# LayerScale with a residual on one Trainium2 core: head blocks of 4 or of 6 rows

## The chip, the cores and the metric

The kernel runs on one core of one Trainium2 chip. Its time is the device time of one execution in microseconds, and the time quoted is the median over several executions. The engines that matter here are the vector engine (DVE), which does the arithmetic, the two engines that issue transfers (SP, the sync engine, and ACT, the scalar engine), and the core's 16 DMA engines, which move the data between the chip's memory (DRAM) and the core's on-chip memory (128 partitions). SP's transfers appear in the profile as queue q1, ACT's as queue q10.

## The reference

```python
B, S, D = 1024, 16, 512
# x and y: [B, S, D] bfloat16; gamma: [D] bfloat16
def reference(x, y, gamma):
    return x + gamma * y
```

Flattened, x and y are 16384 rows of 512 values, 16.78 MB each, and the output has the same size. So 33.56 MB are read and 16.78 MB written, and for each element there is one multiplication and one addition.

## The kernel before

**Tiling.** The 16384 rows are dealt to the 128 partitions, 128 rows to each. In what follows a "row" is a row of one partition: 512 bf16 values, 1 KB. `BLOCKS` (line 7) cuts these 128 rows into three blocks. Within a block, `rows_of` (line 65) gives each partition one stretch of DRAM that has no gaps, as long as the block has rows: partition p of a 64-row block reads 64 KB, and partition p+1 reads the 64 KB after it. The whole of y stays in `y_sb` (128 rows per partition), is multiplied and added to in place, and is stored from there. x passes through the smaller `x_sb`; the last number of an x entry is the row of `x_sb` at which it is put, and an x load that overwrites rows of an earlier one waits until the additions that read those have been done (`frees`, line 102).

**Queues.** The order of the transfers is written out by hand. `SP` (line 12) and `ACT` (line 20) list them as (kind, first row, row behind the last), where kind is y, x, g (gamma) or s (a store). SP issues y rows 0 to 4, y 4 to 68, x 4 to 68, y 68 to 128, x 68 to 120, x 120 to 128. ACT issues x rows 0 to 4, gamma, and then the stores of rows 4 to 68, 0 to 4 and 68 to 128. The first two of SP and the first of ACT (`EARLY`, line 22) are put at the start of the program. What follows them on each engine waits for `HOLD`, the landing of y's head (line 24): the tensor engine waits for it (line 147) and releases SP, ACT and DVE by one semaphore each (line 149). The stores wait for `RELEASE`, the landing of x rows 68 to 120 (line 26), and each for the additions of its rows.

**Arithmetic.** `PIECES` (line 9) cuts the 128 rows into pieces of 8, 16, 44, 52 and 8 rows, one DVE instruction each for the multiplication (line 180) and for the addition (line 189). Piece 0 is rows 0 to 8 and so takes in the head and the beginning of the second block. Before that, gamma's row is spread over the partitions by one matmul with a row of ones (line 152) and copied to `gamma_sb` (line 154). The order of DVE's work is

```python
DVE = [('m', 0), ('m', 1), ('m', 2), ('a', 2), ('a', 0), ('a', 1), ('m', 3), ('m', 4), ('a', 3), ('a', 4)]
```

The addition of piece 2 (rows 24 to 68) comes first of the additions because x rows 68 to 120 are put over the places of x rows 24 to 68 in `x_sb`.

Of the kernel before, what the change touches and what calls it, by code (L numbers as in the profile page):

```python
# [3 lines left out]

BLOCKS = [4, 64, 60]

PIECES = [8, 16, 44, 52, 8]


SP = [
    ('y', 0, 4),
    ('y', 4, 68),
    ('x', 4, 68, 4),
    ('y', 68, 128),
    ('x', 68, 120, 24),
    ('x', 120, 128, 0),
]
ACT = [('x', 0, 4, 0), ('g',), ('s', 4, 68), ('s', 0, 4), ('s', 68, 128)]  # L20

EARLY = (2, 1)

HOLD, AHEAD = ('y', 0, 4), (2, 1)

RELEASE = ('x', 68, 120, 24)

# [10 lines left out]
def kernel(  # L38
# [22 lines left out]
    dt = xf.dtype  # L61
    edges = [sum(BLOCKS[:c]) for c in range(len(BLOCKS) + 1)]
    assert edges[-1] == rows

    def rows_of(t, a, b):

        c = max(c for c in range(len(BLOCKS)) if edges[c] <= a)
        assert b <= edges[c + 1]
# [6 lines left out]
    y_sb = nc.alloc_sbuf_tensor("y_sb", [P, rows, D], dt).ap()  # L75
    x_loads = [w for w in ACT + SP if w[0] == "x"]
    y_loads = [w for w in SP + ACT if w[0] == "y"]
    stores = [w for w in SP + ACT if w[0] == "s"]
    for loads in (x_loads, y_loads, stores):
# [33 lines left out]
    def ring(eng, what, n_early, n_ahead):  # L113

        known, went = 0, False
        for k, w in enumerate(what):
            kind = w[0]
            if k == n_ahead:
                _take(s_held[eng], 1, eng)
            need = frees(w) if kind == "x" else pieces_of(w[1], w[2]) + list(w[3:]) if kind == "s" else []  # L120
            need = max((order[c] + 1 for c in need), default=0)
            if kind == "s" and not went:
                _take(s_go, 1, eng)
                went = True
            if need > known:
                eng.wait_ge(s_add, need)
                known = need
            if kind == "g":
                i = eng.dma_start(out=gamma_row, in_=gamma.unsqueeze(0)).then_inc(s_gamma, 16)
            elif kind == "x":  # L130
                to = x_sb[:, w[3] : w[3] + w[2] - w[1], :]
                i = eng.dma_start(out=to, in_=rows_of(xf, w[1], w[2])).then_inc(s_load[w], 16)
            elif kind == "y":
                r = slice(w[1], w[2])
                i = eng.dma_start(out=y_sb[:, r, :], in_=rows_of(yf, w[1], w[2])).then_inc(s_load[w], 16)
            else:
                r = slice(w[1], w[2])
                i = eng.dma_start(out=rows_of(of, w[1], w[2]), in_=y_sb[:, r, :]).then_inc(s_out, 16)
            if k < n_early:
                early.append(i.ins)  # L140

    ring(nc.sync, SP, EARLY[0], AHEAD[0])
    ring(nc.scalar, ACT, EARLY[1], AHEAD[1])

# [89 lines left out]
```

## Time and profile before

| | |
|---|---|
| median of 3 runs | 119.76 us (119.75 to 119.79) |
| span of the profiled execution | 118.2 us (118.227 in the trace) |
| what lies around the span, if the median is taken for it | 1.53 us |
| DVE busy | 70.1 us |
| bytes moved | 50.33 MB, mean 426 GB/s over the span |

The profile gives for each DMA engine's unit of work (a "packet", here one partition's stretch) its start, its length and its size. Collected by transfer, in the order in which they run, in us from the start of the span:

| transfer | rows | bytes of one packet | packets per DMA engine | first packet starts | last engine done | median packet, ns |
|---|---|---|---|---|---|---|
| load y | 0 to 4 | 4096 | 8 | 1.38 | 3.43 | 159 |
| load x | 0 to 4 | 4096 | 8 | 2.59 | 4.37 | 159 |
| load y | 4 to 68 | 65536 | 8 | 4.03 | 23.89 | 2422 |
| load x | 4 to 68 | 65536 | 8 | 23.41 | 43.23 | 2420 |
| load y | 68 to 128 | 61440 | 8 | 42.75 | 61.38 | 2269 |
| load x | 68 to 120 | 53248 | 8 | 60.90 | 77.09 | 1966 |
| load x | 120 to 128 | 8192 | 8 | 76.65 | 79.55 | 309 |
| store | 4 to 68 | 65536 | 8 | 79.11 | 98.87 | 2418 |
| store | 0 to 4 | 4096 | 8 | 98.43 | 100.11 | 159 |
| store | 68 to 128 | 61440 | 8 | 99.67 | 118.23 | 2267 |

Besides, each transfer ends on each engine with a 4-byte packet of 9 ns, its semaphore. Gamma is a packet of 1024 bytes of 46 ns on one engine, at 9.00, and its semaphore comes at 11.50. Packets that follow each other on an engine overlap by 3 ns in these records where nothing holds them up. "Last engine done" is the end of the slowest engine; the fastest is some 0.33 to 0.47 us earlier throughout, so the next transfer starts on the fast engines before the last one is done on the slow ones.

### The profile page before, as it was taken

The numbers are of one execution on the slowest core, as the hardware profiler recorded it, in microseconds if no ns is written. First come the engines' busy times: TensorE is split into PE (matmuls) and PEld (weight loads), VectorE is DVE, ScalarE is ACT, GpSimd is POOL, SyncE is SP. The second block draws the span as 40 slices with busy tenths as digits, with TensorE's granted clock in tenths as the row PEclk, the third lists the DMA queues.
The fourth block names the chain that finished last, engine by engine and source line by source line (L and its number), as shares of the span: only waits on it lengthen the run. The fifth ranks groups of instructions, "written<-read, shape, count | busy, mean of one in ns | idle before, by whom it ended". The sixth has DMA issues, their size and how long they took to land. (4 is left out here: it accounts for less than half of the span.)

```text
span 118.2 us, 91 instructions
## 1 busy us (share of the span) xinstructions
PE 0.6 (0%) x1; PEld 0.1 (0%) x1; DVE 70.1 (59%) x12; POOL 0.2 (0%) x4
## 2 busy tenths in 40 slices
PE   0000100000000000000000000000000000000000
PEld 0000000000000000000000000000000000000000
DVE  0000200089999969999999999999999900000000
POOL 0000000000000000000000000000000000000000
DMA  6999889988899879879969696898899889799793
GB/s 248 461 666 399 355 355 399 665 355 355 355 599 466 355 333 624 374 333 499 499 288 576 288 576 288 360 637 355 355 576 488 355 355 510 333 582 416 333 499 166
DMA packets 1442, 50.33 MB, mean 426 GB/s; under 512 B 161, under 2 KB 162, under 8 KB 546
## 3 DMA queue, kind: packets, MB, share of 16 engines
q1 hardware_dynamic: 864, 33.03, 64.8%
q10 hardware_dynamic: 578, 17.30, 33.9%
HBM read 33.56 MB, written 16.78 MB: 426 GB/s over the span
## 5 line engine op out<-in xcount | busy, mean ns | idle before, releaser
L180 DVE TENSOR_TENSOR y_sb<-y_sb,gamma_sb 128x4096 bf16<-128x4096 bf16 (+3 forms) x5 | 34.7, 6981 | 10.9 <-DVEq L35 10.9
L189 DVE TENSOR_TENSOR y_sb<-x_sb,y_sb 128x4096 bf16<-128x4096 bf16 (+3 forms) x5 | 34.7, 6981 | 1.2 <-DVEq L35 1.1
L154 DVE CAST gamma_sb<-gamma_ps 128x512 bf16<-128x512 f32 x1 | 0.7, 692 | 10.2 <-DVEq L35 10.2
L146 DVE MEMSET ones_row<- 1x128 bf16 x1 | 0.2, 165 | 2.0 <-PEq L51 2.0
L152 PE MATMUL gamma_ps<-gamma_row,ones_row 1*128 1x512 bf16 x1 | 0.6, 581 | 11.6 <-PEq L35 11.6
L152 PEld LDWEIGHTS gamma_ps<-gamma_row,ones_row 1*128 1x128 bf16 x1 | 0.1, 101 | 11.6 <-issue 11.6
L218 POOL MEMSET const-bfloat16-1.0<- 128x1 bf16 x1 | 0.1, 101 | 0.0
L218 POOL MEMSET const-uint8-127<- 128x1 uint8 x1 | 0.1, 101 | 0.0
L218 POOL MEMSET const-float32-0.0<- 128x1 f32 x1 | 0.1, 98 | 0.2 <-issue 0.2
L218 POOL MEMSET const-float32-1.0<- 128x1 f32 x1 | 0.1, 98 | 0.0
## 6 DMA issues: line engine op xcount, KB each, us to landing
y_sb<-in_y_dram SPq DMA_DIRECT2D x1, 7680.0 KB, 57.3
out_dram<-y_sb ACTq DMA_DIRECT2D x1, 7680.0 KB, 23.8
x_sb<-in_x_dram SPq DMA_DIRECT2D x1, 6656.0 KB, 21.7
x_sb<-in_x_dram SPq DMA_DIRECT2D x1, 1024.0 KB, 22.0
y_sb<-in_y_dram SPq DMA_DIRECT2D x1, 512.0 KB, 3.4
x_sb<-in_x_dram ACTq DMA_DIRECT2D x1, 512.0 KB, 4.2
out_dram<-y_sb ACTq DMA_DIRECT2D x1, 512.0 KB, 22.3
y_sb<-in_y_dram SPq DMA_DIRECT2D x1, 23.4
```

Of the source, the lines that this page charges most:

```text
L146: nc.vector.memset(ones_row, 1.0).then_inc(s_ones, 1)
L152: nc.tensor.matmul(gamma_ps, ones_row, gamma_row, start=True, stop=True).then_inc(s_ps, 1)
L154: nc.vector.tensor_copy(out=gamma_sb, in_=gamma_ps).then_inc(s_dve, 1)
L180: nc.vector.tensor_tensor(out=yt, in0=yt, in1=g, op=MULT).then_inc(s_dve, 1)
L189: nc.vector.tensor_tensor(out=yt, in0=xt, in1=yt, op=ADD).then_inc(s_add, 1)
L218: nc = _bacc.Bacc("TRN2", target_bir_lowering=False, num_devices=1)
```

## The change

The two head blocks grow from 4 rows to 6, and the second block shrinks from 64 rows to 62. The third block stays. The queues' lists follow: y's and x's head are rows 0 to 6, the second block is rows 6 to 68, and `HOLD` is y's new head. `x_sb` keeps its places: x rows 0 to 68 stand at its rows 0 to 68. The pieces of the arithmetic, their order and the rows that they work on stay, and so do the number of transfers on each queue and their order.

```diff
-BLOCKS = [4, 64, 60]
+BLOCKS = [6, 62, 60]
...
 SP = [
-    ('y', 0, 4),
-    ('y', 4, 68),
-    ('x', 4, 68, 4),
+    ('y', 0, 6),
+    ('y', 6, 68),
+    ('x', 6, 68, 6),
     ('y', 68, 128),
     ('x', 68, 120, 24),
     ('x', 120, 128, 0),
 ]
-ACT = [('x', 0, 4, 0), ('g',), ('s', 4, 68), ('s', 0, 4), ('s', 68, 128)]
+ACT = [('x', 0, 6, 0), ('g',), ('s', 6, 68), ('s', 0, 6), ('s', 68, 128)]
...
-HOLD, AHEAD = ('y', 0, 4), (2, 1)
+HOLD, AHEAD = ('y', 0, 6), (2, 1)
```

## The prediction

> **What bounds the kernel now.** I read the page's utilization and queue parts first, then the DMA packets of the trace (tabled by transfer above), then DVE's and the queues' timelines for the slack of everything else.
>
> ```profile
> span 118.2 us, 91 instructions
> PE 0.6 (0%) x1; PEld 0.1 (0%) x1; DVE 70.1 (59%) x12; POOL 0.2 (0%) x4
> q1 hardware_dynamic: 864, 33.03, 64.8%
> q10 hardware_dynamic: 578, 17.30, 33.9%
> HBM read 33.56 MB, written 16.78 MB: 426 GB/s over the span
> ```
>
> The two queues' packets take 64.8 + 33.9 = 98.7% of the time of all 16 DMA engines: 116.7 of 118.23 us. The first packet starts at 1.38 us, so of the rest (1.53 us) all but some 0.15 is the latency of the very first transfer. The DMA engines are the bound from 1.38 us to the last store's semaphore, and only the packets' lengths, or a hole between them, can move the end.
>
> The packets' undisturbed length is a straight line in their size: 159 ns for 4096 bytes, 309 for 8192, 1966 for 53248, 2267 for 61440, 2418 for 65536. Between neighbours that is 0.0366 to 0.0369 ns per byte, and some 8 ns are left for each packet. With these, and 3 ns of overlap per packet, an engine needs 24 x 156 + 24 x 2415 + 16 x 2264 + 8 x 1963 + 8 x 306 = 116.08 us, and 0.06 for its semaphores: 116.14. The slowest engine takes 118.23 - 1.38 = 116.85. So 0.71 us is all that is lost on it, and by the end times most is lost in the first transfers: the last engine is done with both heads at 4.37, where 16 x 156 ns after 1.38 (plus semaphores) would be 3.89: 0.48 us. The rest comes in the second block of y, whose first packets on the 16 engines take 2481 ns on average and up to 2554. From 77 us on nothing is lost: all stores run at 2418, 159 and 2267 ns.
>
> What else could set the end is DVE and the issue of transfers:
>
> ```profile
> 0.00 0.85 SPq L135 DMA_DIRECT2D y_sb<-in_y_dram  x2
> 0.13 0.38 ACTq L132 DMA_DIRECT2D x_sb<-in_x_dram  x1
> ...
> 3.71 0.33 SPq L132 DMA_DIRECT2D x_sb<-in_x_dram  x1
> 3.90 0.50 ACTq L129 DMA_DIRECT2D gamma_row<-in_gamma_dram  x1
> ...
> 12.32 0.69 DVE L154 CAST gamma_sb<-gamma_ps 128x512 bf16<-128x512 f32 x1 [10.16 <-DVEq L35]
> 23.95 18.43 DVE L180 TENSOR_TENSOR y_sb<-y_sb,gamma_sb 128x4096 bf16<-128x4096 bf16 x3 [10.94 <-DVEq L35]
> 43.45 18.43 DVE L189 TENSOR_TENSOR y_sb<-x_sb,y_sb 128x22528 bf16<-128x22528 bf16 x3 [1.08 <-DVEq L35]
> 55.37 2.53 SPq L132 DMA_DIRECT2D x_sb<-in_x_dram  x2
> 61.80 16.22 DVE L180 TENSOR_TENSOR y_sb<-y_sb,gamma_sb 128x26624 bf16<-128x26624 bf16 x2
> 77.41 17.36 ACTq L138 DMA_DIRECT2D out_dram<-y_sb  x3
> 78.17 16.23 DVE L189 TENSOR_TENSOR y_sb<-x_sb,y_sb 128x26624 bf16<-128x26624 bf16 x2
> ```
>
> Columns: start, length, engine, line, what. The reader is to see three slacks. DVE waits 1.08 us for x 4 to 68 before its first addition (43.45). SP issues x 68 to 120 at 55.37, when that addition ends, and the engines come to it at 60.90: 5.5 us, less the 1.4 us that the first transfer took from issue to packet, about 4.1 us of cover. DVE ends at 78.17 + 16.23 = 94.40, the last store is issued then, and the engines come to it at 99.67: 5.3, less 1.4 and the issue, over 3 us of cover.
>
> **The change part by part.** (1) Packet lengths. No 6144-byte or 63488-byte packet is in the trace. Halfway between 4096 and 8192 lies 234 ns, halfway between 61440 and 65536 lies 2342.5. Each engine has 8 packets of y's head, 8 of x's head and 8 of the head's store: 24 x (234 - 159) = +1.80 us. It has 24 packets of the second block: 24 x (2342.5 - 2418) = -1.81 us. Sum: -0.01 us. The number of packets, and so their 8 ns each, stays, and so do the semaphores.
>
> Bounds of this: all sizes in the trace are multiples of 4096 bytes, and the starts of the stretches in DRAM too; 6144 and 63488 are not. If packets of odd size ran as the slowest group of the trace does (2481 against 2418, +63 ns), the 24 long ones cost +1.51 us. The outer end is that each pays for the next multiple, 309 and 2418: 48 x 75 = +3.6 us. Below, the gain is bounded by the 0.71 us that are lost now. I take 0, because five sizes lie on one line and the 60 KB stretches run as fast per byte as the 64 KB ones, in loads and stores.
>
> The Trainium skill has a rule about the odd sizes ("DMA: Bandwidth & Descriptors", How a descriptor splits into AXI transactions): a descriptor is cut into 256-byte transactions, and what doesn't start on a 256-byte boundary or leaves a remainder pays extra. 6144 is 24 x 256, 63488 is 248 x 256, all starts are multiples of 2048, so by the rule the extra is nothing, and the outer end above falls away; no run here shows a packet off the 4096 grid. The same page (Latency and other measured facts) reports slow copies where partitions lie large powers of two apart, from 2 MiB up, and that would speak for leaving 64 KB; the 64 KB stretches at 2418 ns show no such loss here.
>
> (2) The heads. They end 16 x 75 ns = 1.2 us later, at about 5.6 instead of 4.37. The second block of y is issued at 0.43 and ready long before (the first transfer needed 1.38), so it follows at once, as it does now at 4.03. Whether the 0.48 us lost in the start-up stay is open: lost per packet or at the first reads, it stays; if short packets cause it, longer ones lose less. I take it as it is; the ends are 0 and -0.48.
>
> (3) The hold. y's head lands later: its 8 packets alternate with x's from 2.59 on, so I put it at about 4.2 instead of 3.43. Behind the hold on SP are x 6 to 68 and y 68 to 128 (issued at 3.71 and 4.09, then about 4.5 and 4.9); the engines come to the first at about 24. On ACT it is gamma: issued about 0.8 us later, landing at 12.3 to 14.7 instead of 11.50 (one more long packet on its engine at most), the copy done at 13.8 to 16.2 instead of 13.01. DVE's first multiplication is at 24.5. All hidden, with 8 us or more to spare. The stores stand behind the hold too and wait for 77 us anyway.
>
> (4) DVE. y's second block lands 16 x 75 - 8 x 75.5 = +0.60 us later, at 24.48; the multiplications run from 24.55 to 42.98. x's second block ends at the same 43.2, since rows 0 to 68 of both are then through. The wait before the addition shrinks from 1.08 to 0.48 us, and the addition starts at 43.45 as now. If that cover were gone, d us late would meet the 4.1 us ahead of x 68 to 120 and the 3 us ahead of the last store: still nothing.
>
> (5) The stores. Rows 6 to 68 take 0.60 us less (done at 98.26), the head's 0.60 more (100.1), and the last store starts where it does now.
>
> Sum: -0.01 + 0 + 0 + 0 + 0. The span stays 118.2, and with the 1.53 us around it the time is 119.76, the median of the runs (the profiled execution has no time of its own outside its span, so the median stands for it).
>
> **The rivals.** What this kernel's measurement can tell from no change is about 0.2%, 0.24 us.
>
> Slower: the odd packets. Stretches that start off the 4096-byte grid, 62 KB apart, run slower from DRAM than the aligned ones. For it: y's second block has packets of 2481 ns on average in its first round, so reads can be slower than an engine's best. Against it: these are aligned ones; x at 64 KB, y at 60 KB and x at 52 KB are all at the line. It decides from 10 ns for each of the 24 long packets (0.24 us). Its price is 0 to 63 ns; at 31 ns it is +0.75, so 120.5. Chance 0.23, with the outer end of 123.4 in it.
>
> Faster: the start-up loses less. Longer head packets hide the gaps of the start, and stretches 62 KB apart spread the first round of the second block better. For it: the 0.48 us in the heads and the 2481 ns lie exactly where the change is. Against it: the number of packets is the same, and the longest ones (185 to 352 ns) are the first of an engine, which come whatever the size. With most of the 0.71 gone, -0.4: 119.35. Chance 0.14.
>
> A new wait: DVE's later start reaches the end. It needs more than 0.48 us beyond what is worked out, and then over 3 us more. 0.01, at no price that I can find.
>
> The change doesn't move the end: that is the forecast, 0.62.
>
> **How the numbers follow.** Forecast 119.76, within 0.24 us. Its own range, 119.6 to 119.95, is the spread of the start-up: the slowest engine is 0.09 us behind the next one throughout, and such details may fall differently. Faster by over 0.2% 0.14, within 0.62, slower 0.24 (odd packets 0.23, the new wait 0.01). For 8 in 10 the range reaches to 119.45 and to 120.3, which leaves out about 0.07 below and 0.12 above.
>
> **What would show it.** In the profile after: queue shares that still sum to about 98.7%, with 32.77 MB on q1 and 17.56 on q10; packets of 234 and 2342 ns; DVE's first multiplication at 24.55 and its wait before the first addition about 0.48; issue of x 68 to 120 still at 55.4; stores without loss. Wrong it is if 62 KB packets are over 2352 ns, if the second block's first round moves far from 63 ns above the line, or if a hole appears between heads and second block.

## The result and the profile after

The changed kernel takes 120.42 us (median of 5 runs, 120.36 to 120.64) against 119.75 us for the kernel before on the same chip (119.71 to 119.79): a ratio of 1.0062, 95% interval 1.0051 to 1.0073. It is slower by 0.67 us, where no change was forecast. The profiled execution's span grew from 118.23 to 119.10 us, by 0.87. The 0.87 is somewhat too much: the timed runs of the kernel before beside the experiments have spans of 118.3 to 118.8 us, mostly 118.4, so the execution that was profiled before was a short one.

First the page of the changed kernel: the span, the engines, and its two DMA queues (packets, MB, share of the 16 engines' span).

```profile
span 119.1 us, 91 instructions
PE 0.6 (0%) x1; PEld 0.1 (0%) x1; DVE 70.1 (59%) x12; POOL 0.2 (0%) x4
q1 hardware_dynamic: 864, 32.77, 63.9%
q10 hardware_dynamic: 578, 17.56, 34.4%
HBM read 33.56 MB, written 16.78 MB: 423 GB/s over the span
```

The same number of packets and bytes, and two rows per partition have moved from q1 to q10, as they should. The queues' shares sum to 98.3% instead of 98.7%. The engines' work has hardly grown: packet time averaged over the 16 engines is 117.05 us against 116.72, so 0.33 of the 0.87 us is longer packets on the average engine. By the landings of the last store the average engine ends 0.60 us later (118.55 against 117.95) and the slowest 0.87 (119.06 against 118.19). So some 0.27 us is time without packets on the average engine, and another 0.27 that the slowest engine, which sets the end, is 0.52 us behind the mean instead of 0.25.

Now its timeline (start, length, engine, line, what, idle time before).

```profile
0.00 0.84 SPq L135 DMA_DIRECT2D y_sb<-in_y_dram  x2
0.12 0.38 ACTq L132 DMA_DIRECT2D x_sb<-in_x_dram  x1
...
5.97 0.33 SPq L132 DMA_DIRECT2D x_sb<-in_x_dram  x1
...
20.51 0.69 DVE L154 CAST gamma_sb<-gamma_ps 128x512 bf16<-128x512 f32 x1 [18.36 <-DVEq L35]
25.47 18.43 DVE L180 TENSOR_TENSOR y_sb<-y_sb,gamma_sb 128x4096 bf16<-128x4096 bf16 x3 [4.26 <-DVEq L35]
44.33 18.43 DVE L189 TENSOR_TENSOR y_sb<-x_sb,y_sb 128x22528 bf16<-128x22528 bf16 x3 [0.43 <-DVEq L35]
56.25 2.53 SPq L132 DMA_DIRECT2D x_sb<-in_x_dram  x2
...
78.31 17.33 ACTq L138 DMA_DIRECT2D out_dram<-y_sb  x3
```

From the first addition on, every event is 0.87 to 0.90 us behind the kernel before: the first addition (44.33 against 43.45), the issue of x 68 to 120 (56.25 against 55.37), the stores (78.31 against 77.41). DVE still waits for x before its first addition (0.43 us), so it isn't DVE that holds things up. What is late is late already when y's head has landed and SP goes on (5.97 us, against 3.71).

One thing has to be known of the times of packets. In this document, as in the table ahead of the prediction, they are set so that the last packet ends with the span. On the profile's own axis, which the windows below use, they are earlier, by 0.38 us in the kernel before and 0.45 in the changed one (0.36 to 0.45 in the runs below): the first packet starts at 1.00 us there, not at 1.38. Lengths, holes and lags are not touched by this, but a difference between two kernels' packet times can be off by up to 0.1 us.

The windows view tells where the time is lost. Its columns are the stretch in us, its length, the busy time of four engines, the granted clock, the DMA engines' busy share, and GB/s (a packet counts where it starts). First the kernel before, then the changed one, both from 0.3 us after the first packet on:

```profile
1.30:2.30 1.00, 0.00 (x0) 0.00 (x0) 0.17 (x1) 0.00 (x0) 1.00 1.05 406
2.30:3.30 1.00, 0.00 (x0) 0.00 (x0) 0.00 (x0) 0.00 (x0) 1.00 0.99 406
```

```profile
1.30:2.30 1.00, 0.00 (x0) 0.00 (x0) 0.17 (x1) 0.00 (x0) 1.00 0.79 295
2.30:3.30 1.00, 0.00 (x0) 0.00 (x0) 0.00 (x0) 0.00 (x0) 1.00 0.97 381
```

In the first of these microseconds the changed kernel starts 295 KB instead of 406. The packets' own records say more. This is when each of the 16 DMA engines had finished y's head (us, sorted), and when each finished its last store:

```
before   head 3.10 3.12 3.12 3.14 3.17 3.17 3.21 3.21 3.23 3.23 3.28 3.30 3.30 3.34 3.37 3.43
         end  117.79 ... 118.11 118.13 118.13 118.23
changed  head 4.70 4.70 4.70 4.72 4.73 4.73 4.74 4.79 4.83 4.87 4.94 5.04 5.08 5.47 5.67 5.76
         end  118.51 ... 118.61 118.80 119.03 119.10
```

The fast engines are done with y's head 1.6 us later than before, with half as many bytes again and x's longer packets in between. The three slowest fall up to 0.8 us behind the mean, and at the end it is still they that stand apart. If packets that follow each other without a hole are joined to chains, each of the 16 chains of the changed kernel has the same packets, 24 of 62 KB and 24 of 6 KB among them: the work of a late engine isn't taken over by the others. The packets of y's head show the loss: in the kernel before the longest head packet takes 352 ns (159 is the rule), in the changed kernel 1128 ns (234 is the rule), and 19 packets of y's head are over a quarter too long, against 13. From 5.8 us on the slowest engine loses no more than 0.03 us in long packets.

The fast engines pay later. The stores are issued only when x rows 68 to 120 have landed on the slowest engine too (77.96; they are issued at 78.31), and the first store's packets start at 79.63. Eight engines, done with the last x load before that, stand idle for 0.08 to 0.32 us, and the stores then run 0.16 us per engine over their rule on average. In the kernel before there is no such hole, and its stores lose nothing.

### The profile page after: what moved, and what is told of

Same layout as the page of the kernel before. It is cut to its first block, busy times and chain, and to the rows that moved or that the text cites. A ratio compares the mean times of both kernels' runs of the same rounds, so it can differ in the third digit from the quotient of the medians.

```text
span 119.1 us, 91 instructions
## 1 busy us (share of the span) xinstructions
PE 0.6 (0%) x1; PEld 0.1 (0%) x1; DVE 70.1 (59%) x12; POOL 0.2 (0%) x4
```

## The experiments

Three theories were set against each other. **Theory 1**: the time is lost in the first reads of y's head. **Theory 2**: it is lost because x's head packets now alternate with the 62 KB packets; in the changed kernel y's second block is ready when y's head ends, while x's head still has some packets left, and the engines take packets from the two queues in turn, so that x's head lands at 16.0 us instead of 4.4. **Theory 3**: 62 KB packets, which lie off the 4096-byte grid, are slow (the slow rival of the prediction).

In the tables "lag" is the slowest engine's time behind the mean of the 16 when y's head has landed, in the profiled execution (before: 0.20 us; changed, first trace: 0.79). Medians of the kernel before beside these runs were 119.71 to 119.80.

### Is it seen again, and which theory holds?

The changed kernel once more:

> The changed kernel once more. Theory 1 (start-up reads): the added time is lost by the slowest DMA engine in the first packets of y's head (in the first trace one took 1128 ns instead of 234, and its engine stayed 0.8 us behind the mean from 5.8 us on). Then again at least one head packet over 500 ns, an engine late by 0.5 us or more at the landing of y's head, and the time 120.3 to 120.7, with more scatter than before's 119.71 to 119.79. Theory 2 (alternation of x's head with the 62 KB packets) and theory 3 (62 KB packets are slow): the time is the same, 120.4, but whether a long head packet is there does not matter, so the slowest engine may be on time at 5.8 us and lose it later.

Heads of 4 rows with 62 KB packets everywhere else (the rows of x, y, the stores and two pieces follow):

```diff
-BLOCKS = [4, 64, 60]
+BLOCKS = [4, 62, 62]
-PIECES = [8, 16, 44, 52, 8]
+PIECES = [8, 16, 42, 52, 10]
```

> Blocks 4, 62, 62: heads of 4 rows as before, all long packets 63488 bytes (62 KB apart, off the 4096-byte grid). Theory 1: heads as before, so time as before, 119.6 to 119.95. Theory 2: x's head lands by 4.4 us without alternating, so also as before. Theory 3: 40 instead of 24 long packets of 62 KB per engine, so +0.67 x 40/24 = +1.1, about 120.9.

Against the changed kernel, x's head on SP's queue:

```diff
 SP = [
     ('y', 0, 6),
+    ('x', 0, 6, 0),
...
-ACT = [('x', 0, 6, 0), ('g',), ('s', 6, 68), ('s', 0, 6), ('s', 68, 128)]
+ACT = [('g',), ('s', 6, 68), ('s', 0, 6), ('s', 68, 128)]
-EARLY = (2, 1)
+EARLY = (3, 0)
-HOLD, AHEAD = ('y', 0, 6), (2, 1)
+HOLD, AHEAD = ('y', 0, 6), (3, 0)
```

> Blocks 6, 62, 60 with x's head put behind y's head on SP's queue, so that it cannot alternate with the second block; gamma is first on ACT, behind the hold. Theory 1: y's head still begins with 6144-byte reads and some of them are long, so 120.2 to 120.7. Theory 2: x's head lands at 5.3 to 6.2 us instead of 16.0, and the time falls back to 119.6 to 119.95. Theory 3: 120.4.

Heads of 8 rows, with all packets on the 4096-byte grid (6 becomes 8 in all lists):

```diff
-BLOCKS = [6, 62, 60]
+BLOCKS = [8, 60, 60]
```

> Blocks 8, 60, 60: head packets of 8192 bytes and the rest of 61440, all on the 4096-byte grid; x's head (8 packets) alternates with the second block even longer than in the changed kernel. Theory 1, if the size or pitch of 6144 bytes is what collides: the first packets are short again, 119.6 to 119.95; if any longer head collides, 120.4 or more. Theory 2: more packets alternate than with 6 rows, so 120.4 to 121. Theory 3: no 62 KB packets, 119.75.

| run | time, us | ratio to before (95%) | lag, us |
|---|---|---|---|
| changed, again | 120.51 | 1.0073 (1.0061 to 1.0085) | 0.78 |
| blocks 4, 62, 62 | 119.75 | 1.0013 (0.9996 to 1.0030) | 0.18 |
| one queue for both heads | 120.53 | 1.0077 (1.0065 to 1.0089) | 0.85 |
| blocks 8, 60, 60 | 120.06 | 1.0031 (1.0019 to 1.0042) | 0.32 |

Theory 3 falls: with 40 packets of 62 KB per engine instead of 24 there is no change that can be told from none; their median is 2342 ns, on the line through the other sizes. Theory 2 falls too. These are the landings of the two heads (transfer, queue, KB, us from issue to landing), in the changed kernel

```profile
y_sb<-in_y_dram SPq DMA_DIRECT2D x1, 768.0 KB, 5.6
x_sb<-in_x_dram ACTq DMA_DIRECT2D x1, 768.0 KB, 15.8
```

and in the run with one queue:

```profile
y_sb<-in_y_dram SPq DMA_DIRECT2D x1, 768.0 KB, 4.6
x_sb<-in_x_dram SPq DMA_DIRECT2D x1, 768.0 KB, 6.0
```

With one queue x's head no longer waits for long packets, and the time is the same 120.5. What all three executions with 6-row heads have in common is three late engines (the trace doesn't name them, so whether they are the same three is not shown): 5.47, 5.67, 5.76 us (the other thirteen by 5.08); again 5.10, 5.41, 5.47 (the others by 4.70); with one queue 4.19, 4.54, 4.60 (the others by 3.68). Theory 1 holds so far. With 8 rows a smaller loss remains, between the two times that were expected, and no engine stands out.

### Is it that short packets come first?

If the first reads lose because they are short, they should not be the first. Long packets first, shown against the changed kernel; the run with 4 rows has the same edit:

```diff
 SP = [
-    ('y', 0, 6),
     ('y', 6, 68),
...
-ACT = [('x', 0, 6, 0), ('g',), ('s', 6, 68), ('s', 0, 6), ('s', 68, 128)]
+ACT = [('g',), ('y', 0, 6), ('x', 0, 6, 0), ('s', 6, 68), ('s', 0, 6), ('s', 68, 128)]
-EARLY = (2, 1)
+EARLY = (1, 1)
-HOLD, AHEAD = ('y', 0, 6), (2, 1)
+HOLD, AHEAD = ('y', 0, 6), (3, 3)
```

> Blocks 6, 62, 60, but the 62 KB load of y goes first on SP; gamma, y's head and x's head follow on ACT and alternate with the long packets; SP holds only x 68 to 120 back. All packets are those of the changed kernel. Theory 1 (what is lost is lost because the very first reads are short packets that collide): the 0.8 us come back, 119.3 to 119.8, and the slowest engine is at most 0.4 us behind the mean. If long first packets collide as well, or 6 KB packets are slow wherever they run: 120.3 or more.

> The same order with blocks 4, 64, 60. Theory 1: the 0.48 us that the kernel before loses in its heads come back in part, 119.3 to 119.75, and equal to the run with blocks 6, 62, 60 within 0.15. If the start loses the same whatever runs first: 119.75.

With 6 rows: 121.91 us, 1.0180 (1.0165 to 1.0195). With 4 rows: 121.94, 1.0185 (1.0171 to 1.0199). Both expectations missed, and theory 1 in that form falls: long packets lose more. The first load's packets take 3366 and 3667 ns at most, where 2342 and 2418 are the rule, and over the whole load an engine's packets run 0.70 and 0.79 us over their rule on average, against 0.09 for y's head of 4 rows in the kernel before. In the same runs the 6144-byte loads ran at 234 ns at most once they came among long ones: it isn't their size that is slow; being first is what these runs leave.

There is a second lesson in these two runs. y's head, for which gamma's matmul waits, landed only at 27.4 us, and DVE came late with it. The timeline of the run with 6 rows:

```profile
48.73 18.43 DVE L188 TENSOR_TENSOR y_sb<-x_sb,y_sb 128x22528 bf16<-128x22528 bf16 x3
60.65 2.53 SPq L131 DMA_DIRECT2D x_sb<-in_x_dram  x2
```

The first addition starts 5.28 us later than in the kernel before, more than the cover of 4.1 us that the prediction worked out ahead of x 68 to 120. That load is issued at 60.65, its first packet starts at 61.99, and the first engine had been done with y 68 to 128 at 61.25: a hole of at least 0.74 us on that engine, and of 0.88 us on the average of the 16. Behind the hole, where engines again start close together, the packets of that load are too long once more: up to 2935 ns instead of 1966, 0.58 us per engine. The run with 4 rows has a mean hole of 0.89 us and loses 0.70 behind it. In the kernel before the same load lost 6 ns.

### What is read first, or where it lies?

Against the changed kernel, the head loads take rows 0 to 4 only, so that 4096-byte packets are read 6144 bytes apart:

```diff
 SP = [
-    ('y', 0, 6),
+    ('y', 0, 4),
     ('y', 6, 68),
+    ('y', 4, 6),
+    ('x', 4, 6, 4),
     ('x', 6, 68, 6),
...
-ACT = [('x', 0, 6, 0), ('g',), ('s', 6, 68), ('s', 0, 6), ('s', 68, 128)]
+ACT = [('x', 0, 4, 0), ('g',), ('s', 6, 68), ('s', 0, 6), ('s', 68, 128)]
-HOLD, AHEAD = ('y', 0, 6), (2, 1)
+HOLD, AHEAD = ('y', 0, 4), (2, 1)
```

> Blocks 6, 62, 60, but the head loads take rows 0 to 4 only: 4096-byte packets that lie 6144 bytes apart; rows 4 to 6 of y and x follow behind the hold as two more loads of 2048-byte packets, which cost an engine 2 x (8 x 8 + 9) ns = 0.15 us more. If the distance of 6144 bytes between partitions makes the first reads collide: several engines late by 0.4 us or more at the landing of the head, time 120.4 to 120.8. If the length of the packets does: the head is as in the kernel before (slowest engine within 0.3 us of the mean), time 119.8 to 120.0.

Against that, the same loads from a 4-row and a 2-row block:

```diff
-BLOCKS = [6, 62, 60]
+BLOCKS = [4, 2, 62, 60]
-ACT = [('x', 0, 4, 0), ('g',), ('s', 6, 68), ('s', 0, 6), ('s', 68, 128)]
+ACT = [('x', 0, 4, 0), ('g',), ('s', 6, 68), ('s', 0, 4), ('s', 4, 6), ('s', 68, 128)]
```

> Blocks 4, 2, 62, 60, the loads in the same order and with the same packets as in the run that took rows 0 to 4 out of a 6-row block (120.78): only the place in DRAM differs, the head's 4096-byte packets lie 4096 bytes apart instead of 6144. One more store (8 packets of 2 KB) costs 0.07 us. Theory 1a (the first reads of all 16 engines, which start together, collide by where they lie): head on time as in the kernel before, time 119.75 + 0.15 + 0.07 = 119.9 to 120.1. Theory 1b (it is the length of the head or the number of transfers at the start): 120.6 to 120.9.

The first: 120.78 us, 1.0079 (1.0066 to 1.0093), lag 0.96. The second: 119.89, 1.0015 (1.0006 to 1.0024), lag 0.16. This is the pair that decides. Loads, packets, queues and order are the same, and the second kernel even has a store more; only the addresses in DRAM differ, and 0.9 us lie between them. The landings of the two heads, 6144 apart:

```profile
y_sb<-in_y_dram SPq DMA_DIRECT2D x1, 512.0 KB, 4.6
x_sb<-in_x_dram ACTq DMA_DIRECT2D x1, 512.0 KB, 5.5
```

and 4096 apart:

```profile
y_sb<-in_y_dram SPq DMA_DIRECT2D x1, 512.0 KB, 3.5
x_sb<-in_x_dram ACTq DMA_DIRECT2D x1, 512.0 KB, 4.4
```

Their windows from 0.3 us after the first packet on, 6144 apart:

```profile
1.30:2.30 1.00, 0.00 (x0) 0.00 (x0) 0.17 (x1) 0.00 (x0) 1.00 0.93 266
2.30:3.30 1.00, 0.00 (x0) 0.00 (x0) 0.00 (x0) 0.00 (x0) 1.00 0.83 336
```

and 4096 apart:

```profile
1.30:2.30 1.00, 0.00 (x0) 0.00 (x0) 0.17 (x1) 0.00 (x0) 1.00 0.93 352
2.30:3.30 1.00, 0.00 (x0) 0.00 (x0) 0.00 (x0) 0.00 (x0) 1.00 1.00 397
```

In the first, the DMA engines are as busy as in the second (0.93), but start 266 KB instead of 352: their packets are open longer. Three engines are late once more (4.14, 4.62 and 4.66 us, the others by 3.87). At the landing of x's head the slowest engine is at 5.59 us in the first and at 4.66 in the second, some 0.9 us apart; the spans differ by 0.84.

The same with 8-row blocks, 4096-byte packets 8192 apart (edits as in the first of the pair, with 8 for 6):

> Blocks 8, 60, 60, head loads of rows 0 to 4 only: 4096-byte packets that lie 8192 bytes apart; rows 4 to 8 follow behind the hold as two loads of 4096-byte packets (2 x (8 x 8 + 9) ns = 0.15 us more). If the distance alone decides, the first reads collide as with full 8-row heads: time 120.06 + 0.15 = 120.1 to 120.3. If length does: head as in the kernel before, 119.9.

121.33 us, 1.0135 (1.0120 to 1.0151), lag 0.60, far worse than the 120.1 to 120.3 that the distance alone would have given. Here x's head is hit as well: its packets run 0.54 us per engine over the rule, 79 of 128 by more than a quarter. x's head lands 5.9 us after its issue:

```profile
x_sb<-in_x_dram ACTq DMA_DIRECT2D x1, 512.0 KB, 5.9
```

That is at 6.07 us, some 1.4 behind the kernel with 4-row and 2-row blocks; the spans differ by 1.43. Less was read from the 8-row block than in the run with full 8-row heads, and more was lost: the addresses matter, but no simple count of rows or bytes gives the loss.

Two more sizes (6 becomes 5 or 7 in all lists):

```diff
-BLOCKS = [6, 62, 60]
+BLOCKS = [5, 63, 60]
```

> Blocks 5, 63, 60: head packets of 5120 bytes, 5120 apart. If the loss grows step by step with distance and length: 120.0 to 120.2, slowest engine 0.3 to 0.5 us behind the mean. If 6144 is special: as before, 119.7 to 119.9. If everything off the 4096-byte grid collides: 120.4 or more.

```diff
-BLOCKS = [6, 62, 60]
+BLOCKS = [7, 61, 60]
```

> Blocks 7, 61, 60: head packets of 7168 bytes, 7168 apart. If the loss grows step by step: between the runs with 6 rows (120.4 to 120.5) and 8 rows (120.06) it has no order, so 120.3 would say only that the distance decides irregularly; off the grid collides: 120.4 or more; 6144 special: about 120.0 or less.

With 5 rows 119.94 us, 1.0018 (1.0009 to 1.0027), lag 0.41; with 7 rows 120.10, 1.0035 (1.0023 to 1.0048), lag 0.41. So heads of 5, 7 and 8 rows cost 0.2 to 0.4 us, and 6 rows 0.7 to 0.8: there is a loss that all longer heads have, and one that this head has besides. The time with 5 rows fell between what was expected of a loss that grows step by step (120.0 to 120.2) and of one that only 6 rows have (119.7 to 119.9). "Off the 4096-byte grid" explains neither (8 is on it).

### The distance or the place?

The head block is put behind the other two in x, y and out, with its distance kept; the same edit for 4 rows is the control:

```diff
-        block = t[P * edges[c] : P * edges[c + 1]].rearrange("(p n) d -> p n d", p=P)
+        first = (edges[c] - edges[1]) % rows
+        block = t[P * first : P * (first + BLOCKS[c])].rearrange("(p n) d -> p n d", p=P)
```

> Blocks 6, 62, 60, but the head's rows lie behind the other two blocks in DRAM (in x, y and out alike), packets and distances unchanged. If the distance of 6144 bytes decides: three engines late by 0.4 us or more at the landing of y's head again, 120.3 to 120.7. If the absolute place does: another pattern of late engines, or none, and the time moves away from 120.4, down to 119.75 if none is late.

> Blocks 4, 64, 60 with the head's rows behind the other blocks in DRAM. If the distance of 4096 bytes decides: as the kernel before, 119.6 to 119.95, slowest engine within 0.3 us of the mean. If the absolute place decides: engines late by 0.4 us, 120.1 or more.

The head of 6 rows at the end: 120.08 us, 1.0027 (1.0017 to 1.0038), lag 0.41. The head of 4 rows at the end: 119.80, 1.0006 (0.9997 to 1.0015), lag 0.16. The same two windows with 6 rows:

```profile
1.30:2.30 1.00, 0.00 (x0) 0.00 (x0) 0.17 (x1) 0.00 (x0) 1.00 0.85 283
2.30:3.30 1.00, 0.00 (x0) 0.00 (x0) 0.00 (x0) 0.00 (x0) 1.00 0.97 406
```

The first microsecond is as poor as in the changed kernel (283 and 295 KB), the second as good as in the kernel before (406). With the place, half of the loss has gone, and the three late engines with it: y's head is done at 4.57 to 5.28 us without a gap in between. The other half stays, as with heads of 5, 7 and 8 rows. With the distance alone the time would have stayed at 120.3 to 120.7; without any late engine it would have been 119.75. The measured 120.08 lies between, so distance and place both count, that is, the addresses. (The other two blocks move too, by the size of the head block. The control moves its blocks in the same way and stays within the noise of the kernel before.)

### x's head late

Against the kernel before:

```diff
-ACT = [('x', 0, 4, 0), ('g',), ('s', 4, 68), ('s', 0, 4), ('s', 68, 128)]
+ACT = [('g',), ('x', 0, 4, 0), ('s', 4, 68), ('s', 0, 4), ('s', 68, 128)]
-EARLY = (2, 1)
+EARLY = (2, 0)
-HOLD, AHEAD = ('y', 0, 4), (2, 1)
+HOLD, AHEAD = ('y', 0, 4), (2, 0)
```

> Blocks 4, 64, 60, with x's head issued on ACT behind the hold and behind gamma, so that its 8 packets alternate with y's 64 KB packets and y's head runs alone. Theory 1: y's head is read as before, 119.6 to 119.9. Theory 2 (alternation costs): as in the changed kernel, 120.2 or more. If the second block of y is not ready when y's head ends (about 2.8 us), a hole of up to 1.2 us opens: up to 121.

119.81 us, 1.0004 (0.9995 to 1.0013). x's head lands 29.1 us after its issue, its packets alternating with long ones, and the time can't be told from the kernel before: once more against theory 2. The hole that was thought possible does not open: y's second block starts at 2.98 us, right behind y's head.

No version that was run beats the kernel before; three equal it within the noise.

## Why the prediction was wrong

**Step 2, the heads, is what failed.** Its term was 0, and the runs show +0.7 us in its place, lost in the first reads of y's head. It took the 0.48 us that are lost at the start "as it is" and set the ends at 0 and -0.48: it saw that the loss lies in the heads, and then allowed it only to shrink. The runs show that it depends on what is read first and where that lies, and that it can grow: 0.2 to 0.4 us more for heads of 5, 7, 8 rows (or 6 at the end of the tensors), 0.7 to 0.8 for these 6 rows, 2.1 with long packets first, the hole behind them included. A sign of it stood in the trace: y's second block, where the engines come into long packets close together, has first packets of up to 2554 instead of 2418 ns, and the packets of the very first load take up to 352 instead of 159. The prediction used the former only as a price for long packets wherever they run. As a bound these 0.14 and 0.19 us would still have been too small.

**The slow rival had the wrong place.** It made the 62 KB packets slow, all 24 of them; they are at 2342 ns in the loads, as step 1 said, and a kernel with 40 of them was not slower. That its price of 120.5 lies close to the measured 120.42 is chance. The fast rival (the start-up loses less) named the right place with the wrong sign.

**Step 1, the packets' lengths, was right.** Medians are 234 and 2342 ns. This is also what the Trainium skill's rule makes of sizes that are multiples of 256 bytes ("DMA: Bandwidth & Descriptors", How a descriptor splits into AXI transactions). The same page's figures for distances between partitions (Latency and other measured facts, HBM row pitch at large powers of two) begin at 512 KiB; here distances of 4 to 8 KB made a difference, at the start of the stream.

**Steps 3 to 5, what is hidden, did not set the end, though the sizes were off.** SP's held loads were issued at 5.97 us, not 4.5: y's head landed at 5.76, not at 4.2, by the late engines and because x's longer packets take turns with it. Gamma landed at 19.76, not at 12.3 to 14.7: x's head had packets left when the long ones began, and gamma stood behind them on ACT's queue, each waiting for a 2.3 us packet in turn. That was missed altogether, and the copy to `gamma_sb` came only 4.3 us ahead of its use instead of some 8. It cost nothing: DVE waited for y until 25.47 (predicted 24.55) and for x for 0.43 us (predicted 0.48). Step 5 left out that the stores wait for the slowest engine's x load: hence the holes of up to 0.32 us on the fast engines, which did not move the end.

**The sum** was -0.01 + 0 and should have been -0.01 + 0.9 for the slowest engine: at the landing of y's second block it stands at 25.40 us, where step 4 had 24.48. In the timed runs the change is 0.67, in the profiled executions 0.87. Two figures around the sum were off, without an effect on the forecast: the time outside the span is some 1.3 us in every timed run, not 1.53, and the first transfer takes 1.00 us from issue to packet on the profile's axis, not 1.38. The start of the changed kernel differs from one execution to the next (its longest head packet took 1128 ns in one trace and 796 in the other), but its times do not scatter more for that: 120.50 to 120.77 when it was run again, where 17 runs of the kernel before beside it span 119.58 to 120.09.

Why these addresses collide when 16 engines begin to read them, and why on three engines, no run here shows. That the loss in the first reads depends on addresses is shown by the pair with equal loads and by the move of the block; what in the memory makes the packets wait is open.

## What to carry to other kernels

Where the DMA engines are busy from end to end, the end belongs to the slowest of them, and here the engines that fell behind in the first packets were still last at the end: compare the 16 engines, and not their mean alone. The first load of this kernel has its own price, up to some 1.4 us more than in the kernel before, which depends on where its rows lie in DRAM; measure it for each layout, and set a bound for it on the losing side too. In the two runs with a hole in the stream the hole cost more than its length (0.88 and 0.89 us, and 0.58 and 0.70 us more in the load behind it). That this comes from the engines starting together again fits the first load, but no run separates it.

## What the runs showed of the hardware that was not expected

- Reads that run at one speed in the middle of a stream (2342 ns per 62 KB packet, 234 ns per 6 KB packet) took up to 3366 and 1128 ns in the load with which all 16 DMA engines began.
- Equal loads of 4096-byte packets differed by 0.9 us of kernel time, by their addresses alone (119.89 and 120.78).
- Packets of two queues were taken in turn, one by one, though one queue's had 6 KB and the other's 62 KB: a 768 KB load beside 62 KB packets landed at 15.8 us from its issue instead of 6.0, and the two kernels took the same 120.5 us.
